# A filter contraction by channel quads, with selection matmuls in place of small relayout DMAs

## The chip, the cores and the metric

The kernel runs on one core of a Trainium2 chip. The metric is device time in microseconds (us); every time below is a median of three to seven runs. A profile gives the span of one run, which is about 1.8 us shorter than that run's time.

The runs fell on several chips, of two kinds. The kernel before took 367.5 to 368.0 us on two of them and 372.6 to 373.1 us on the others. So times of different sets are compared through the kernel before of the same set. A ratio is the mean time of one kernel's fast runs over that of the other's of the same rounds, so it is not quite the ratio of the medians that are quoted.

## The reference

Two branches share the input `u` (2048 x 640) and are mixed by a gate. Branch A builds a filter K for each of 640 channels from 128 complex modes and convolves it with `u` by way of spectra; branch B is a gated MLP.

```python
P = jnp.exp(logdA[:, :, None] * l[None, None, :])
K = jnp.einsum("dn,dnl,dn->dl", Cc, P, dB).real      # 640 channels x 2048
Kf = rfft(pad(K)); Uf = rfft(pad(u^T))               # cut: written with rfft2
y = irfft(Uf * Kf)[..., :L]^T + u * Dskip
b = (gelu(x @ w_gate) * (x @ w_up)) @ w_down
return g * y + (1 - g) * b
```

The kernel factors a position as l = X1 + X2, with 32 values of X1 and 21 of X2 (denser near the start, so K is computed at 672 points rather than at each of the 2048 positions), so that K of one channel is a 32 x 21 matrix, the product of a 128 x 32 and a 128 x 21 matrix over the 128 modes. There is a cosine and a sine part: two accumulating matmuls for each channel.

## The kernel before

All work is declared with a guessed duration and a lane (`pe` TensorE, `ac` ScalarE, `ve` VectorE, `dma` the Sync queue, `pool` GpSimd's). A planner then fixes the order on every engine from a `script` (the order of ScalarE's table functions) and a `prio` table (a priority for each lane). The order was found by search for this one kernel. Each engine and each DMA queue works strictly in its order.

The contraction, in chunks of 160 channels, four chunks, which run in two stretches of two:

```python
def contract(ch):
    c0 = CH * (ch % 2)
    for hb in range(2):
        def go(hb=hb):
            for g in range(GH):                       # 20
                for q in range(2):                    # cosine, sine
                    for j in range(4):                # one channel in each quarter of the columns
                        d = c0 + G4 * j + GH * hb + g
                        nc.tensor.matmul(ps[32 * j:32 * j + 32, 6 + hb, NX2 * g:NX2 * g + NX2],
                                         lhsT=cs1[ch % 2][:, q, :, d - c0],
                                         rhs=cs2[ch % 2][:, q, :, d - c0], start=(q == 0), stop=(q == 1))
        pe(160 * 20, go, ...)
    kst = at(O_KST + 1696 * (ch % 2), [128, NX2, G4], BF16, "kst")
    for hb in range(2):
        ac(actns(NX2 * GH), lambda hb=hb: nc.scalar.copy(...))          # PSUM to kst, 420 elements
    for j in range(4):
        for q in range(4):                                              # 16 small DMAs per chunk
            na = 6 if q == 0 else 5
            f = dma if j < 2 or ch < NCH - 1 else pool
            e = nc.sync if j < 2 or ch < NCH - 1 else nc.gpsimd
            f(410, lambda j=j, q=q, na=na, e=e: e.dma_start(
                out=Kt[32 * q:32 * q + 32, 0:na, CH * ch + G4 * j:CH * ch + G4 * j + G4],
                in_=kst[32 * j:32 * j + 32, q:NX2:4, :]), ..., lane="kt", prio=1)
```

`Kt` is the layout in which the spectrum matmuls read K. The Sync queue carries those DMAs (planned at 410 ns each), and also the MLP's weights, and the tables FK of K's spectrum:

```python
Wg = [at(O_W + 1280 * k, ...) for k in range(2)]
Wu = [at(O_W + 2560 + 1280 * k, ...) for k in range(2)]
... dma(430, go, w=[k], lane="w", x=KB160)                      # weights of MLP tile f
... dma(430, lambda i0=i0, n=n: nc.sync.dma_start(out=FK[:, i0:i0 + n]..., in_=dFK[...]), lane="fkl")
```

## Time and profile before

The kernel before takes 372.5 us (371.55 to 372.64). Its recorded profile has a span of 364.8 us, so its run took about 366.6 us. Where stages are compared in numbers, I therefore use two later runs on one and the same chip, called before_again (span 367.2) and after_again (span 349.4).

| kernel before, profile of span 364.8 us | |
|---|---|
| first contraction stretch | 106.3 to 123.4 us |
| second contraction stretch | 191.6 to 210.7 us |
| first K-spectrum matmul | 219.8 us |
| from there to the end (VectorE's spectrum products bind) | 145.0 us |

The page's costliest groups: busy us and the mean ns of one; then the idle time of the engine just before them and what ended it. The contraction's line has 1280 matmuls, with 15.2 us of idle time that no visible wait explains ("issue").

```profile
PE 304.6 (84%) x3014; PEld 180.6 (50%) x3014; DVE 297.8 (82%) x526; ACT 217.1 (60%) x333; POOL 21.2 (6%) x39
...
L514 PE MATMUL ps<-arena 128*32 128x21 bf16 x1280 | 21.0, 214 | 15.2 <-issue 15.2
```

TensorE's timeline in the first stretch (start, duration, then the idle time before in brackets) shows the shape of that idle time: after a first group of 240 pairs, 128 pairs of weight load and matmul, 256 instructions, take 2.1 us, and then nothing runs for 1.3 to 2.2 us.

```profile
106.28 3.71 PE L514 MATMUL ps<-arena 128*32 128x21 bf16 x240
111.28 2.14 PE L514 MATMUL ps<-arena 128*32 128x21 bf16 x128 [1.29 <-issue]
115.01 2.07 PE L514 MATMUL ps<-arena 128*32 128x21 bf16 x128 [1.59 <-issue]
118.74 2.09 PE L514 MATMUL ps<-arena 128*32 128x21 bf16 x128 [1.66 <-issue]
123.01 0.42 PE L514 MATMUL ps<-arena 128*32 128x21 bf16 x16 [2.19 <-issue]
```

The Trainium skill, "Advanced Engine Details and Errata", ISA Cache, gives an instruction cache line as 16 KB, 256 instructions. The trace agrees: the stops come every 256 instructions, and the instruction queue's transfers are 16 KB each (23 of them in this run).

The Sync queue's own timeline (L527 is the relayout DMA, L321 a weight load, L793 an FK load):

```profile
113.28 22.86 SPq L527 DMA_DIRECT2D arena<-arena  x32
136.24 0.54 SPq L321 DMA_DIRECT2D arena<-in_B_w_up_dram  x1
136.83 1.09 SPq L321 DMA_DIRECT2D arena<-in_B_w_gate_dram  x2
...
198.26 0.80 SPq L793 DMA_DIRECT2D arena<-dFK  x2
199.15 19.03 SPq L527 DMA_DIRECT2D arena<-arena  x24
218.22 1.06 SPq L793 DMA_DIRECT2D arena<-dFK  x2
```

The 32 relayout DMAs hold the queue for 22.86 us, 0.71 us each on average, not the planned 0.41. The waits between 124 and 182 us (engine, line, what it waited for: us in total, times, longest):

```profile
DVE arena L590 <- PE ps L586: 12.8, 10, 4.7
ACT arena L572 <- PE ps L568: 10.0, 10, 2.6
...
PE ps L568 <- DMA arena<-in_B_w_gate_dram: 2.8, 1, 2.8
```

### The profile page before, as it was taken

What the parts mean: (1) busy time and instruction counts of PE and PEld (TensorE: products, weight loads), DVE (VectorE), ACT (ScalarE), POOL (GpSimd) and SP (SyncE); (2) the same over time, 40 slices, a digit from 0 to 9 for tenths busy, and PEclk for the clock granted to TensorE, in tenths of its full rate; (3) what the DMA queues carried; (4) which work ended last, traced back from release to release, by engine and by line L of the source; (5) the groups of instructions that cost most, each with busy time, mean ns of one, the idle gap of its engine ahead of it and who ended that gap; (6) DMA issues with size and microseconds to landing.
All of it is one profiled execution on the core that took longest, in us unless ns stands there. A gap on an engine that the chain in (4) does not pass through costs nothing.

```text
span 364.8 us, 7365 instructions
## 1 busy us (share of the span) xinstructions
PE 304.6 (84%) x3014; PEld 180.6 (50%) x3014; DVE 297.8 (82%) x526; ACT 217.1 (60%) x333; POOL 21.2 (6%) x39
## 2 busy tenths in 40 slices
PE   0056669999995796999997397999999999999985
PEld 0012123444564442444446354667677777777654
DVE  8599599968893395898698613999999999998962
ACT  5899599999999567459991046999421011100000
POOL 6000000000000000000046050000000000000000
PEclk9999899999997598999997589999999999999999
DMA  7754523020200113020745524014520003001311
GB/s 151 191 102 102 133 115 106 18 55 20 56 20 13 21 21 73 2 55 18 217 151 142 162 32 161 2 39 136 101 44 2 18 20 90 20 18 46 102 65 62
DMA packets 63585, 26.42 MB, mean 72 GB/s; under 512 B 56832, under 2 KB 60864, under 8 KB 63168
## 3 DMA queue, kind: packets, MB, share of 16 engines
q1 hardware_dynamic: 62912, 24.54, 26.5%
q0 software_dynamic: 640, 1.42, 1.5%
q8 instruction: 23, 0.38, 0.4%
q14 instruction: 10, 0.08, 0.1%
HBM read 12.83 MB, written 6.03 MB: 52 GB/s over the span
## 4 chain that ended last, share of the span: by engine, by line
DVE 36%; PE 27%; ACT 18%; issue 8%; SPq 7%; DMA 3%; POOL 0%; DVEq 0%; ACTq 0%; POOLq 0%
DVE arena L881 28%; PE ps L586 9%; PE ps L568 7%; SPq L298 6%; PE ps L514 6%; ACT arena L461 4%; ACT arena L426 3%; ACT arena L572 3%; DVE arena L860 2%; PE ps L992 2%; DVE arena L1001 2%; ACT arena L361 2%; ACT arena L637 2%; PE ps L823 2%; ACT L572 1%
## 5 line engine op out<-in xcount | busy, mean ns | idle before, releaser
L881 DVE TENSOR_TENSOR arena<-arena 128x640 bf16<-128x640 bf16 (+5 forms) x112 | 106.6, 1006 | 2.3 <-ACT arena L975 0.9
L568 PE MATMUL ps<-arena 128*128 128x512 bf16 x280 | 70.7, 400 | 31.2 <-DMA arena<-in_A_u_dram 28.0
L586 PE MATMUL ps<-arena 128*128 128x512 bf16 x260 | 62.0, 389 | 0.5 <-DVE arena L590 0.4
L971 PE MATMUL ps<-arena 128*128 128x320 bf16 x448 | 62.0, 299 | 0.4 <-ACT arena L849 0.4
L568 PEld LDWEIGHTS <-arena 128*128 128x128 bf16 x280 | 28.2, 101 | 68.3 <-issue 32.4
L590 DVE TENSOR_TENSOR arena<-ps,arena 128x512 bf16<-128x512 f32 x52 | 35.0, 686 | 27.4 <-PE ps L586 26.4
L975 ACT ACTIVATE arena<-ps,omg 128x640 bf16<-128x640 f32 x16 | 12.7, 794 | 67.9 <-PE ps L971 61.0
L971 PEld LDWEIGHTS <-arena 128*128 128x128 bf16 x448 | 43.6, 98 | 17.2 <-issue 0.6
L461 ACT ACTIVATE arena<-arena 128x2240 bf16<-128x2240 int16 (+1 forms) x20 | 43.1, 2175 | 4.8 <-DVE arena L454 4.7
L586 PEld LDWEIGHTS <-arena 128*128 128x128 bf16 x260 | 25.9, 100 | 33.4 <-issue 5.3
L992 PE MATMUL ps<-arena 128*128 128x320 bf16 x256 | 37.7, 299 | 2.3 <-DVE arena L1001 1.2
L572 ACT ACTIVATE arena<-ps 128x512 bf16<-128x512 f32 (+1 forms) x56 | 29.2, 614 | 10.1 <-PE ps L568 10.0
L514 PE MATMUL ps<-arena 128*32 128x21 bf16 x1280 | 21.0, 214 | 15.2 <-issue 15.2
L992 PEld LDWEIGHTS <-arena 128*128 128x128 bf16 x256 | 24.7, 98 | 12.3 <-issue 3.3
L514 PEld LDWEIGHTS <-arena 128*32 128x32 bf16 x1280 | 20.0, 153 | 16.9 <-issue 16.9
L849 ACT CAST arena<-ps 128x640 bf16<-128x640 f32 (+1 forms) x40 | 21.2, 616 | 3.3 <-DVE arena L881 1.6
L452 DVE SCALAR_TENSOR_TENSOR arena<-arena 128x160 int32<-128x160 f32 x84 | 20.7, 316 | 2.0 <-ACT arena L461 2.0
L827 ACT ACTIVATE arena<-ps 128x640 bf16<-128x640 f32 x32 | 20.0, 805 | 3.8 <-PE ps L823 3.8
L843 PE MATMUL ps<-arena 128*128 128x320 bf16 x144 | 21.1, 299 | 1.2 <-ACT arena L849 0.5
L823 PE MATMUL ps<-arena 128*128 128x320 bf16 x128 | 20.4, 309 | 1.3 <-ACT arena L849 1.3
L785 POOL DMA_INDIRECT arena<-in_A_u_dram,i_u x8 | 9.5, 1190 | 181.9 <-ACT arena L461 179.8
L1001 DVE SCALAR_TENSOR_TENSOR arena<-ps,g_f,arena 128x640 bf16<-128x640 f32 x16 | 14.0, 876 | 6.5 <-PE ps L996 6.5
(87 smaller groups left out, 304.0 us busy)
## 6 DMA issues: line engine op xcount, KB each, us to landing
out_dram<-arena SPq DMA_DIRECT2D x16, 160.0 KB, 1.8
dFK<-arena SPq DMA_DIRECT2D x9, 256.0 KB, 2.0
arena<-in_B_w_gate_dram SPq DMA_DIRECT2D x13, 160.0 KB, 2.9
arena<-in_B_w_up_dram SPq DMA_DIRECT2D x13, 160.0 KB, 2.8
arena<-in_B_w_down_dram SPq DMA_DIRECT2D x13, 160.0 KB, 3.8
arena<-in_A_u_dram SPq DMA_DIRECT2D x4, 320.0 KB, 4.3
dTAB<-arena SPq DMA_DIRECT2D x1, 1024.0 KB, 4.3
arena<-dTAB SPq DMA_DIRECT2D x1, 1024.0 KB, 4.8
```

Source lines behind the costliest of these rows:

```text
L298: dma(1050, lambda: nc.sync.dma_start_transpose(out=xT[tq][:, kt, :], in_=u2[S * tq:S * tq + S, kt * 128:kt * 128 + 128]), w=[("xT", tq, k ...
L461: ac(actns(2 * n * w), lambda: nc.scalar.activation(out=dst, in_=ph.bitcast(I16)[:, :, :, 0:2 * w:2], func=ACT.Sin, scale=SIN_SCALE), r=[( ...
L514: nc.tensor.matmul(ps[32 * j:32 * j + 32, 6 + hb, NX2 * g:NX2 * g + NX2], lhsT=cs1[ch % 2][:, q, :, d - c0], rhs=cs2[ch % 2][:, q, :, d - ...
L568: nc.tensor.matmul(ps[:, k, :], lhsT=Wg[f % 2][:, kt, :], rhs=xT[tq][:, kt, :], start=(kt == 0), stop=(kt == NKT - 1))
L572: ac(actns(512), lambda: nc.scalar.activation(out=HT[f][0:p, tq, :], in_=ps[0:p, k, :], func=ACT.Gelu_apprx_tanh), r=[("bank", k)], w=[("H ...
L586: nc.tensor.matmul(ps[:, 4 + k, :], lhsT=Wu[f % 2][:, kt, :], rhs=xT[tq][:, kt, :], start=(kt == 0), stop=(kt == NKT - 1))
L590: ve(tt(512, 1) + 60, lambda: nc.vector.tensor_tensor(out=HT[f][:, tq, :], in0=ps[:, 4 + k, :], in1=HT[f][:, tq, :], op=ALU.mult), r=[("ba ...
L823: nc.tensor.matmul(ps[:, k + h, 0:DH], lhsT=tab[:, j, q, fsl(ft)], rhs=src[:, j, h * DH:(h + 1) * DH], start=(j == 0), stop=(j == 1))
L881: nc.vector.tensor_tensor(out=out, in0=a, in1=b, op=op)
L971: nc.tensor.matmul(ps[:, k + h, 0:DH], lhsT=HT[f][:, c, 128 * j:128 * j + 128], rhs=Wd[f][:, h * DH:(h + 1) * DH], start=(f == 0), stop=(f ...
L992: nc.tensor.matmul(ps[:, k + h, 0:DH], lhsT=tab[:, ft, q, 128 * j:128 * j + 128], rhs=U[ft][:, q, c, h * DH:(h + 1) * DH], start=(ft == 0 ...
L1001: ve(stt(640) + 50, lambda: nc.vector.scalar_tensor_tensor(out=osb[o].rearrange("p (h d) -> p h d", h=2), in0=ps[:, k:k + 2, 0:DH], scalar ...
```

## The change

The intent: channels k = 4g..4g+3 become one matmul pair, with all four channels' 32 columns as 128 columns of weights and all four channels' 21 columns as 84 moving columns. Of the 4 x 4 blocks of the result only the diagonal ones are wanted. There are 320 pairs in place of 1280. Each accumulator of five quads is copied to a staging tile, and 16 matmuls with 0/1 selection matrices (a "relay") pick the diagonal blocks and put them in `Kt`'s layout, from where two copies write `Kt`. No DMA is left in this path. All exponent, phase and sine tiles change to a quad-major layout for it, and the order (`script` and `prio`) was searched anew.

```diff
+    sj = cp.tile([128, 4, 32], BF16, name="sj")           # 0/1 selection
...
-    cs1 = [at(O_CS1 + 20480 * c, [128, 2, 32, CH], BF16, f"cs1{c}") for c in range(2)]
-    cs2 = [at(O_CS2 + 13440 * c, [128, 2, NX2, CH], BF16, f"cs2{c}") for c in range(2)]
+    cs1 = [at(O_CS1 + 20480 * c, [128, 2, NQD, 128], BF16, f"cs1{c}") for c in range(2)]
+    cs2 = [at(O_CS2 + 13440 * c, [128, 2, NQD, 4 * NX2], BF16, f"cs2{c}") for c in range(2)]
... (exponentials, phases, sines and products write and read the new layout: cut)
-            (the contraction, two copies and 16 DMAs per chunk, shown above)
+    kst = at(O_KST, [128, 4 * NX2, NQD // 2], BF16, "kst")
+        for h in range(2):
+            for s in range(4):
+                def go(k=k, k0=k0):
+                    for g in range(5):
+                        for q in range(2):
+                            nc.tensor.matmul(ps[:, k, 84 * g:84 * g + 84], lhsT=cs1[c][:, q, k0 + g, :],
+                                             rhs=cs2[c][:, q, k0 + g, :], start=(q == 0), stop=(q == 1))
+                pe(10 * 38, go, ...)
+                ac(actns(420), lambda k=k, s=s: nc.scalar.copy(
+                    out=kst[:, :, 5 * s:5 * s + 5], in_=ps[:, k, 0:420].rearrange("p (g e) -> p e g", e=84)), ...)
+            def relay(k=k):
+                for q in range(4):
+                    na = 6 if q == 0 else 5
+                    for j in range(4):
+                        o = ps[32 * q:32 * q + 32, k, 0:480].rearrange("p (a j g) -> p a j g", a=6, j=4)[:, 0:na, j, :]
+                        nc.tensor.matmul(o, lhsT=sj[:, j, :], rhs=kst[:, 4 * q + j:4 * NX2:16, :], start=True, stop=True)
+            def back(k=k, ds=ds):
+                for p, a0, a1 in ((128, 0, 5), (32, 5, 6)):
+                    nc.scalar.copy(out=Kt[0:p, a0:a1, ds]..., in_=ps[0:p, k, 80 * a0:80 * a1]...)
...
-    script = [("trig", 8), ("exp", 6), ("sqrt", 1), ...]
-    prio = {("ACT", "copy"): 2, ..., ("PE", "gate"): 7, ("PE", "k"): 3, ("SP", "w"): 8, ...}
+    script = [("exp", 1), ("trig", 9), ("exp", 5), ("sqrt", 1), ...]
+    prio = {("ACT", "copy"): 1, ..., ("PE", "gate"): 0, ("PE", "k"): 4, ("SP", "w"): 3, ...}
```

## The prediction

> **What bounds the kernel now.** The chain of waits, in order of time, shows: 44 to 88 us mostly ScalarE table functions and copies; 88 to 158 us nearly all TensorE (gate, up, K contraction); 159 to 186 us ScalarE again (sine, gelu, exp, table loads); 191.6 to 220 us the second K contraction and its hand-over. From 226 us VectorE's spectrum products bind; the change leaves that tail alone.
>
> The 1280 contraction matmuls (weights 128x32, 21 columns) occupy TensorE from 106.3 to 123.4 us and from 191.6 to 210.7 us (timeline), 36 us, although they run at 16 ns each: 128 take 2.07 us and are followed by 1.3 to 4.1 us of "issue" (groups by line: 15.2 us in all). I read these gaps as instruction supply, 256 instructions per stop. The second contraction is followed by small relayout DMAs, which hold the Sync queue for 19.0 us (199.2 to 218.2) and push the FK table's loads behind them. First K-spectrum matmul: 219.8 us.
>
> **Removed.** 1280 pairs become 320, with full 128-column weights and 84 columns. The Trainium skill, "TensorE: Matmul & The Clock Gate", Back-to-back issue gap, gives N/2.4 + 2.5 ns; the trace agrees for 320 columns (16 matmuls in 2.17 us, 136 ns). Estimate: 37.5 ns each, 12 us in all, too slow a rate for instruction supply to bind. The 64 DMAs go.
>
> **Added.** 128 selection matmuls, about 1 us per relay of 16 (estimate from about 105 columns), 8 us. ScalarE: 24 more PSUM copies of 420 elements at 506 ns (12.1 us) and 8 writes back, about 0.7 us each (5.7 us, estimated from the copies). TensorE loses about 16 us, ScalarE gains 18 us. Element counts stay; I expect VectorE and ScalarE means unchanged within 5% (inner runs of four keep 8 bytes together).
>
> **How much is critical.** TensorE was nearly saturated from 42 to 191.6 us; there about 5 us are saved (17.2 to 12), but ScalarE, 97% busy from 80 to 120 us, takes 9 us of new work; it has slack only from 120 to 160 us (63% busy). So the second contraction should start 3 us earlier, at about 188 us. It becomes a serial loop between TensorE and ScalarE: four copies, relay, write back, with one staging tile and two PSUM banks, about 4.6 us per half chunk, 18 us for four, 23 us where the clock falls to half: hardly shorter than 19.0 us. The gain comes after it: about 5.5 us to the first K-spectrum matmul in place of 9.1. Sum: 3 + (19.0 - 20) + 3.6 + 1 for FK, so 6 to 7 us.
>
> **Predicted:** 366 us, 8 in 10 within 358.5 to 372.5. Faster by over 2%: 0.43; within 2%: 0.52; slower by over 2%: 0.05.
>
> **What would show it.** Contraction pairs at 37 to 45 ns without 1.3 us issue gaps; ScalarE busy up by 17 to 19 us; first K-spectrum matmul at 210 to 216 us; the tail after it within 2 us of 145 us; in the last contraction ScalarE waiting 1.2 to 2 us for each relay. Exponential (454 ns), sine (2065, 2339 ns) and product (1314, 1486 ns) means unchanged.
>
> **What would make it wrong.** Runs of four slowing ScalarE or VectorE (106 exponentials: 20% would be 10 us of ScalarE); half clock through the whole last contraction; TensorE queued behind a 2 us sine for a bank; or a re-tuned order that hides the copies completely (10 to 14 us faster).

## The result, and the profile after

The kernel after takes 357.86 us (357.65 to 358.82), the kernel before 372.57 us in the same rounds: ratio 0.9619, 95% interval 0.9591 to 0.9648. The result is correct. That is 14.7 us of gain, where 6.5 was predicted.

| us from the span's start | before_again | after_again | difference | predicted |
|---|---|---|---|---|
| second contraction starts | 192.4 | 182.0 | -10.4 | -3 |
| its length, to the last matmul (before) or write back to Kt (after) | 19.9 | 17.6 | -2.3 | +1 |
| from there to the first K-spectrum matmul | 9.9 | 6.1 | -3.8 | -3.6 |
| from there to the end | 145.0 | 143.7 | -1.3 | -1 (FK) |
| span | 367.2 | 349.4 | -17.8 | -6.5 |

Both traces are of one chip; the medians there are 367.61 and 351.18 us, and the run of before that was traced was a slower one of its set. The second contraction's start on TensorE's timeline, before_again and then after_again:

```profile
192.40 3.45 PE L514 MATMUL ps<-arena 128*32 128x21 bf16 x216
```

```profile
182.03 0.92 PE L524 MATMUL ps<-arena 128*128 128x84 bf16 x20
```

The answering lines of the page after, first of its costliest groups. L529 is the staging copy; its mean was to be 506 ns.

```profile
PE 299.7 (84%) x2182; PEld 175.8 (49%) x2182; DVE 297.8 (84%) x528; ACT 237.2 (67%) x374; POOL 15.7 (4%) x32
...
L529 ACT CAST arena<-ps 128x420 bf16<-128x420 f32 x32 | 20.3, 674 | 10.9 <-PE ps L524 6.9
```

TensorE's timeline in the first stretch: pieces of the contraction (L524) and relays (L540) alternate with the MLP's matmuls (L606), and no idle time is listed.

```profile
111.25 0.92 PE L524 MATMUL ps<-arena 128*128 128x84 bf16 x20
112.00 2.45 PE L606 MATMUL ps<-arena 128*128 128x512 bf16 x10
114.59 0.40 PE L540 MATMUL ps<-arena,sj 128*32 128x120 bf16 x16
114.92 0.55 PE L524 MATMUL ps<-arena 128*128 128x84 bf16 x10
```

Twenty contraction matmuls take 0.92 us and ten 0.54 to 0.55, so one more takes (0.92 - 0.55) / 10 = 37 ns. The Trainium skill, "TensorE: Matmul & The Clock Gate", Back-to-back issue gap, gives N/2.4 + 2.5 ns for the gap of an isolated matmul, 37.5 ns for 84 columns, and warns that it counts too little for pairs with weight loads (81 ns at 128 columns). These are such pairs, and the trace keeps to the formula without that addition.

The Sync queue: weights (L325) go out when their buffers are free, and the FK loads (L816) are not behind anything.

```profile
113.27 6.96 SPq L325 DMA_DIRECT2D arena<-in_B_w_up_dram  x2
120.28 1.35 SPq L325 DMA_DIRECT2D arena<-in_B_w_gate_dram  x2
127.32 11.69 SPq L325 DMA_DIRECT2D arena<-in_B_w_up_dram  x2
...
194.35 2.60 SPq L816 DMA_DIRECT2D arena<-dFK  x4
```

The waits between 124 and 182 us: the wait for gate weights is down to 0.4 us (on the weight-load side; it was 3.8 there before), and the gelu's wait for TensorE, 10.0 us before, is no longer listed.

```profile
ACT arena L529 <- PE ps L524: 1.2, 3, 0.6
...
PEld L588 <- DMA arena<-in_B_w_gate_dram: 0.4, 1, 0.4
```

The same stretches in windows, first before_again, then after_again (window, its length, then busy us of TensorE, its weight loads, VectorE, ScalarE, GpSimd; the granted clock; DMA share; GB/s). From 137 to 182 us ScalarE was busy 33.54 of 45 us before, and 44.81 after: the new order fills it.

```profile
109.00:137.00 28.00, 20.94 (x524) 13.02 (x520) 16.41 (x38) 20.43 (x27) 0.00 (x0) 0.76 0.14 17
137.00:182.00 45.00, 41.17 (x181) 17.96 (x182) 35.06 (x75) 33.54 (x46) 0.00 (x0) 0.96 0.29 74
```

```profile
109.00:137.00 28.00, 27.44 (x311) 15.46 (x315) 25.74 (x62) 24.70 (x35) 0.00 (x0) 1.00 0.14 31
137.00:182.00 45.00, 41.85 (x186) 18.44 (x189) 41.74 (x82) 44.81 (x61) 4.01 (x4) 1.00 0.33 90
```

Summed from 60 us to the start of the second contraction, ScalarE's idle time falls from 20.0 us (of 132.4) to 3.9 us (of 122.0), although it does 5.7 us more work there.

The serial loop of the second contraction is as it was foreseen, in after_again: copy, matmuls, relay, write back (L547), at full clock.

```profile
188.57 0.54 PE L524 MATMUL ps<-arena 128*128 128x84 bf16 x10 [0.47 <-ACT arena L529]
189.20 0.71 ACT L529 CAST arena<-ps 128x420 bf16<-128x420 f32 x1 [0.17 <-PE ps L524]
189.96 0.40 PE L540 MATMUL ps<-arena,sj 128*32 128x120 bf16 x16 [0.85 <-ACT arena L529]
190.29 0.55 PE L524 MATMUL ps<-arena 128*128 128x84 bf16 x10
190.47 0.60 ACT L547 CAST arena<-ps 128x400 bf16<-128x400 f32 x2 [0.56 <-PE ps L540]
```

### The profile page after: what moved, and what is told of

It is laid out like the page before. It is cut to its first block, busy times and chain, and to the rows that moved or that the text cites. A ratio compares the mean times of both kernels' runs of the same rounds, so it can differ in the third digit from the quotient of the medians.

```text
span 355.9 us, 5682 instructions
## 1 busy us (share of the span) xinstructions
PE 299.7 (84%) x2182; PEld 175.8 (49%) x2182; DVE 297.8 (84%) x528; ACT 237.2 (67%) x374; POOL 15.7 (4%) x32
## 4 chain that ended last, share of the span: by engine, by line
DVE 38%; PE 27%; ACT 19%; SPq 10%; issue 4%; DMA 1%; another core or an unknown queue 0%; DVEq 0%; ACTq 0%
DVE arena L904 28%; PE ps L588 10%; PE ps L606 8%; SPq L302 7%; ACT arena L466 5%; ACT arena L529 3%; PE ps L524 3%; DVE arena L883 3%; ACT arena L592 3%; PE ps L1015 2%; ACT arena L430 2%; SPq L307 2%; DVE arena L1024 2%; PE ps L846 2%; ACT arena L660 2%
## 5 line engine op out<-in xcount | busy, mean ns | idle before, releaser
L588 PE MATMUL ps<-arena 128*128 128x512 bf16 x280 | 68.5, 396 | 25.9 <-DMA arena<-in_B_w_gate_dram 21.8
L606 PE MATMUL ps<-arena 128*128 128x512 bf16 x260 | 62.3, 382 | 3.2 <-DVE arena L610 3.0
L588 PEld LDWEIGHTS <-arena 128*128 128x128 bf16 x280 | 27.9, 101 | 61.7 <-DMA arena<-in_B_w_gate_dram 22.2
L994 PEld LDWEIGHTS <-arena 128*128 128x128 bf16 x448 | 43.6, 98 | 17.2 <-issue 0.6
L606 PEld LDWEIGHTS <-arena 128*128 128x128 bf16 x260 | 24.8, 99 | 33.4 <-issue 7.2
L1015 PEld LDWEIGHTS <-arena 128*128 128x128 bf16 x256 | 24.7, 98 | 12.7 <-issue 3.7
L529 ACT CAST arena<-ps 128x420 bf16<-128x420 f32 x32 | 20.3, 674 | 10.9 <-PE ps L524 6.9
L420 ACT ACTIVATE arena<-arena 128x320 bf16<-128x320 f32 x64 | 23.3, 465 | 0.0
L883 DVE TENSOR_TENSOR arena<-arena 128x640 bf16<-128x640 bf16 (+1 forms) x30 | 11.1, 419 | 12.9 <-ACT arena L872 12.9
L850 ACT ACTIVATE arena<-ps 128x640 bf16<-128x640 f32 x32 | 20.1, 813 | 1.6 <-PE ps L846 1.6
L655 PE MATMUL ps<-arena 128*128 128x512 bf16 x42 | 13.6, 450 | 8.6 <-ACT arena L660 8.1
```

Source lines behind the costliest of these rows:

```text
L420: nc.scalar.activation(out=e1[:, :, 4 * r:4 * r + 4], in_=quads(aT[:, ds]), func=ACT.Exp, scale=float(sg * (4 + 8 * i)))
L529: ac(actns(420), lambda k=k, s=s: nc.scalar.copy(out=kst[:, :, 5 * s:5 * s + 5], in_=ps[:, k, 0:420].rearrange("p (g e) -> p e g", e=84)), ...
L588: nc.tensor.matmul(ps[:, k, :], lhsT=Wg[f % 2][:, kt, :], rhs=xT[tq][:, kt, :], start=(kt == 0), stop=(kt == NKT - 1))
L606: nc.tensor.matmul(ps[:, 4 + k, :], lhsT=Wu[f % 2][:, kt, :], rhs=xT[tq][:, kt, :], start=(kt == 0), stop=(kt == NKT - 1))
L994: nc.tensor.matmul(ps[:, k + h, 0:DH], lhsT=HT[f][:, c, 128 * j:128 * j + 128], rhs=Wd[f][:, h * DH:(h + 1) * DH], start=(f == 0), stop=(f ...
L1015: nc.tensor.matmul(ps[:, k + h, 0:DH], lhsT=tab[:, ft, q, 128 * j:128 * j + 128], rhs=U[ft][:, q, c, h * DH:(h + 1) * DH], start=(ft == 0 ...
```

## The experiments

The first question was where the surplus of 8 us came from. Two theories: the new contraction alone made the gain (A), or the new order alone did (C).

### Same chip: both kernels, and each half of the change alone

before_again and after_again are the two kernels, unchanged, to have both traces from one chip.

> The kernel before, unchanged, to get a second trace. Its timed runs give 372.5 us, but its first trace has a span of 364.8 us, while the changed kernel's time is only 1.8 us over its span. So the first trace should not show an ordinary run. Theory A (instruction supply): time 372, span 370 to 371, and the 6 us more than in the first trace lie in the two stretches of contraction matmuls, which together take 41 to 43 us in place of 36. Theory B (another place: start, clock or the tail): the two stretches take 35 to 37 us and the 6 us are found before 106 us or after the first K-spectrum matmul.

Measured: 367.85 us, ratio 0.9998 (0.9934 to 1.0061). Neither theory's time came: this chip was faster, and the two stretches take 17.2 + 19.9 = 37.1 us.

> The changed kernel, unchanged, on the same chip: 357.5 to 359 us, span 1.8 us less, first K-spectrum matmul at 212 to 214 us. Both theories expect this; a second trace shows how far its stages move from run to run.

Measured: 351.18 us, ratio 0.9555 (0.9494 to 0.9616): 6 us below what was expected, and the first K-spectrum matmul comes at 205.7 us, not at 212 to 214.

new_k_old_order has the new contraction with the old script and priorities; old_k_new_order is the reverse:

```diff
# new_k_old_order, against after
-    script = [("exp", 1), ("trig", 9), ...];  prio = {...}      # new
+    script = [("trig", 8), ("exp", 6), ...];  prio = {...}      # old
# old_k_new_order, against before
-    script, prio: old
+    script, prio: new, and ("POOL", "kt"): 6, ("SP", "kt"): 5 for the relayout DMAs
```

> The new contraction and relay with the old ScalarE script and the old lane priorities. Theory A (the contraction itself made the gain): 358 to 363 us. Theory C (the re-tuned order made most of it): 367 to 373 us, since ScalarE's 18 us of new copies then stand in an order made without them.

Measured: 372.52 us, ratio 1.0128 (1.0051 to 1.0205). The second contraction starts at 203.4 us, 11.0 later than before; ScalarE's idle time ahead of it stays at 19.8 us (20.0 before) while its work grows by 11.2 us.

> The old contraction and its DMAs with the new script and priorities. Theory A: 370 to 376 us, no better than before. Theory C: 360 to 366 us.

Measured: 378.02 us, ratio 1.0259 (1.0184 to 1.0335). The second contraction starts at 200.2 us. ScalarE's idle time ahead of it is 29.4 us.

So each half alone loses 5 and 10 us, and both together win 16. Neither theory holds by itself. One rival was not tested: each order was searched for its own kernel, and no run shows what a further search with the old contraction would win.

### One part of the order alone

```diff
# new_k_old_script_new_prio, against after          # new_k_new_script_old_prio, against after
-    script = [new]                                 -    prio = {new}
+    script = [old]                                 +    prio = {old}
```

> The new contraction, the old ScalarE script, the new lane priorities. The whole order was worth 21 us on the new contraction (372.5 against 351.2 us). Theory: the script is what fills ScalarE, so this stays near the old order, 365 to 373 us, ratio 0.99 to 1.015. Rival: the priorities did it, 351 to 358 us, ratio below 0.975.

Measured: 383.17 us, ratio 1.027 (1.0242 to 1.0298); second contraction from 214.2 us. That is slower than either expectation.

> The new contraction, the new script, the old priorities. Theory (script): within 6 us of the changed kernel, ratio 0.955 to 0.975. Rival (priorities): 365 us or more, ratio over 0.99. If both mixed kernels are slow, script and priorities only work together.

Measured: 373.86 us, ratio 1.0047 (0.9996 to 1.0097); second contraction from 200.1 us. With both mixed kernels slow, script and priorities also win only together.

### Which engine is full after the change

copies_twice makes every staging copy twice, matmuls_twice every contraction matmul.

```diff
# copies_twice
-                ac(actns(420), lambda k=k, s=s: nc.scalar.copy(...), ...)
+                def stage(k=k, s=s):
+                    for _ in range(2):
+                        nc.scalar.copy(...)
+                ac(actns(420), stage, ...)
# matmuls_twice
-                    for g in range(5):
+                    for g in [x for y in range(5) for x in (y, y)]:
```

> The changed kernel with each of its 32 staging copies made twice (same values, same order, planned as before). It adds 32 times about 0.5 us = 16 us to ScalarE alone, half of it before the second contraction. Theory S (ScalarE has no slack left from 60 us to the K spectrum): 14 to 18 us over the changed kernel, a ratio to before of 0.995 to 1.01, and the second contraction starts 7 to 9 us later than 182 us. Theory T (TensorE bounds the middle and ScalarE still has slack there): 8 to 10 us, ratio 0.978 to 0.988, and the second contraction starts within 3 us of 182 us.

Measured: 375.07 us, ratio 1.0067 (1.0046 to 1.0088), so 17 us over after (357.86 on the same kind of chip) for 20.4 us more ScalarE work (busy 257.6 in place of 237.2). The second contraction starts 9 us later.

> The changed kernel with each of its 320 contraction matmuls made twice (same result, same order). It adds 12 us to TensorE alone, 6 us before the second contraction. Theory S: 1 to 5 us over the changed kernel, ratio to before 0.96 to 0.972. Theory T: 8 to 12 us, ratio 0.978 to 0.99.

Measured: 367.38 us, ratio 0.9866 (0.9836 to 0.9895), 9.5 us over after for about 12 us more TensorE work (an estimate: 320 times the 37 ns read above). The second contraction starts 6 us later.

Both hold: neither engine has much room for more work. That doubling a cost hurts does not show that halving it helps, as the next runs proved.

### Shorter staging copies

The staging copy takes 674 ns and not the 506 ns of the copy before. It writes runs of five elements, the old one runs of 20. plain_staging lets it write one contiguous run; the relay's matmuls then read with a stride.

```diff
-    kst = at(O_KST, [128, 4 * NX2, NQD // 2], BF16, "kst")
+    kst = at(O_KST, [128, NQD // 2, 4 * NX2], BF16, "kst")
-                    out=kst[:, :, 5 * s:5 * s + 5], in_=ps[:, k, 0:420].rearrange("p (g e) -> p e g", e=84)),
+                    out=kst[:, 5 * s:5 * s + 5, :], in_=ps[:, k, 0:420].rearrange("p (g e) -> p g e", e=84)),
-   rhs=kst[:, 4 * q + j:4 * NX2:16, :]
+   rhs=kst[:, :, 4 * q + j:4 * NX2:16].rearrange("p g a -> p a g")
```

> The kernel after, with the staging tile laid out quad-major, so that each of the 32 staging copies writes one contiguous run of 420 elements (it reads the accumulators in their order) and the relay's matmuls read the tile with a stride. Theory: the copy's extra length (674 ns measured against 506 ns of the copy it replaced) comes from its strided access; the mean falls to 480-560 ns, ScalarE loses some 4 to 6 us of work, and as ScalarE has no slack before the second contraction the time falls by 3 to 5 us against the kernel after (ratio to before 0.948 to 0.956 where after gives 0.962; 0.943 to 0.949 on a chip where after gives 0.9555). Rival: the relay's 16 matmuls, 0.40 us with contiguous columns, slow to over 1 us with strided ones and sit in the serial loop, or the copy stays above 600 ns: no gain over 1 us.

Measured: 359.68 us, ratio 0.9661 (0.9595 to 0.9726): no gain. The copies took 508 ns, as the theory had it, but the rival is right: a relay takes 1.06 us in place of 0.40. staging_by_fives keeps both short, with one block of the staging tile for each copy, contiguous, in which the relay finds its runs of five:

```diff
-    kst = at(O_KST, [128, 4 * NX2, NQD // 2], BF16, "kst")
+    kst = at(O_KST, [128, 4, 4 * NX2, 5], BF16, "kst")
-                    out=kst[:, :, 5 * s:5 * s + 5], ...
+                    out=kst[:, s, :, :], ...
-   rhs=kst[:, 4 * q + j:4 * NX2:16, :]
+   rhs=kst[:, :, 4 * q + j:4 * NX2:16, :].rearrange("p s a g -> p a s g")
```

It ran with the kernel after beside it on one chip (after_third), which is the base of that set.

> The kernel after, unchanged, on the chip of the runs beside it, as their base: ratio to before 0.955 to 0.963.

Measured: 351.38 us (350.67 to 353.29), ratio 0.9558 (0.9483 to 0.9633).

> The kernel after, with the staging tile in four blocks, one for each staging copy: each copy writes one contiguous run of 420 elements (508 ns in plain_staging), and the relay's matmuls still read runs of five neighbouring elements, as they do after. Theory that the copy's short runs cost 0.17 us each and that ScalarE has no slack: copies at 500-520 ns, a set of 16 relay matmuls stays at 0.40-0.45 us, and the time falls by 3 to 5 us against the kernel after on this chip (two copies a half lie on the serial path of the last contraction, 16 before it are in the full stretch). Rival that TensorE's order alone sets the second contraction's start: 0 to 1.5 us. Third outcome, relay matmuls slow again because their runs are now split in four: over 0.8 us a set and no gain.

Measured: 349.85 us (348.74 to 351.46), ratio 0.9498 (0.942 to 0.9576): 1.5 us faster than after_third by the medians, and the ranges overlap. The groups show the copy of plain_staging and of staging_by_fives, in this order:

```profile
L529 ACT CAST arena<-ps 128x420 bf16<-128x420 f32 x32 | 15.4, 508 | 14.0 <-PE ps L524 9.7 <-issue 2.5 <-remote 1.7
```

```profile
L529 ACT CAST arena<-ps 128x420 bf16<-128x420 f32 x32 | 15.2, 507 | 7.6 <-PE ps L524 7.3
```

and TensorE's timeline one relay of each, again in this order:

```profile
205.73 1.06 PE L540 MATMUL ps<-arena,sj 128*32 128x120 bf16 x16 [0.65 <-ACT arena L529]
```

```profile
197.72 0.47 PE L540 MATMUL ps<-arena,sj 128*32 128x120 bf16 x16 [0.65 <-ACT arena L529]
```

The copy of staging_by_fives still reads its accumulator with a stride, so it is the short written runs that cost, not the reading. But the expectation of 3 to 5 us for 5 us less ScalarE work was too high. The windows suggest why. In the first contraction's stretch (109 to 137 us) TensorE is the full engine (27.44 of 28 us, ScalarE 24.70); ScalarE is full only after it (44.81 of 45 us), where no staging copy lies. The copies' saved time in the first stretch becomes idle time (ScalarE 23.07 us busy in staging_by_fives) and the second contraction starts only 0.6 us earlier. Adding 10.8 us of copies there overflows the 3.3 us of room; taking 2.7 us away wins nothing. In the second contraction the write back ends 1.3 us earlier (198.9 us; 200.2 in after_third), but the first K-spectrum matmul only 0.1 us: between them, TensorE's spectrum matmuls of `u` take turns with ScalarE's copies of them.

### Accumulator banks and VectorE's help after the second contraction

four_banks lets the first spectrum stages rotate through four pairs of accumulator banks where they had two. helps_banks2 does this and moves some of their copies to VectorE, which is idle there.

```diff
# both
-                k = two(4 if ft else 2)
+                k = two(4 if ft or b else 2)
-                k = two(4 if ft or 1 in hs else 2)
+                k = two(4)
# helps_banks2 also
+                if ft == 0 and q == 1:
+                    ve(tt(640, 1) + 60, lambda ...: nc.vector.tensor_scalar(out=dst, in0=src2, scalar1=1.0 / S, ...), lane="kcp", ...)
+                on_v = ft == 0 and hs == [0] and q == 1           # and the K-spectrum's copies likewise
```

> The kernel after, with a few accumulator copies of the first spectrum stages moved from ScalarE to VectorE where that is idle before its first product (about 12.8 us), and four accumulator pairs in rotation instead of two there. Theory that ScalarE and TensorE together are the limit before the second contraction, without slack: ScalarE work of about 5 us goes away, TensorE waits less for banks; the time falls by 2 to 4 us against the kernel after. Rival: the same order of heads is bound by something else (VectorE's products), no gain: within 1 us of after.

Measured: 353.78 us, ratio 0.9486 (0.9425 to 0.9548), against 0.9619 (357.86 us) for after on the same kind of chip: 4 us faster by the medians, 5 by the ratios. That is a little more than expected, and in another place: the second contraction starts no earlier (184.1 us; 182.6 after). The time is won behind it: from its start to the first K-spectrum matmul 26.1 us (29.6 after), and 142.3 us from there to the end (143.8 after).

> The kernel after, with four accumulator pairs in rotation instead of two for two of the spectrum stages, nothing moved to VectorE. If the banks alone made the gain of helps_banks2 (about 4 to 5 us against after): 3 to 5 us faster than after. If VectorE's share of the copies made it: within 1 us of after.

Measured: 349.25 us, ratio 0.9483 (0.9412 to 0.9555), 2.1 us under after_third: between the two expectations. The banks alone give about half; that VectorE's copies give the rest is inferred across two kinds of chip, and no run moves the copies alone.

### What the old contraction cost in the old order

before_half_contraction leaves out half of the contraction's matmuls. It gives a wrong filter.

```diff
-                    for q in range(2):
+                    for q in range(1):
-                                             ..., start=(q == 0), stop=(q == 1))
+                                             ..., start=True, stop=True)
```

> The kernel before with half of the contraction matmuls of each channel left out (wrong result on purpose), order and all else unchanged. If the contraction's own time is paced by the number of its instructions, its two stretches fall from 17 and 19 us to about 8.5 and 10 us, the idle time that the contraction's line shows with no named wait falls from 15-16 us to 7-8 us, and as the stretches' instructions are shared with the heads' work only part is on the chain. Theory that the old contraction held up the whole TensorE order: the time falls by 14 to 18 us (ratio 0.953 to 0.962). Rival, that only the last stretch is on the chain: by 9 to 11 us (ratio 0.970 to 0.976).

Measured: 367.66 us, ratio 0.9858 (0.9786 to 0.993), 5.4 us: both expectations were too high. The first stretch fell from 17.2 to 8.7 us and the second from 19.9 to 12.2. The first has the expected size, but 3.8 us of it is now a wait for ScalarE's copy. The idle time without a named wait fell over both only from 16.1 to 13.5 us (7 to 8 expected): on this slower kind of chip the second stretch is cut into bursts of some five matmuls. It starts only 2.2 us earlier, and although the first K-spectrum matmul comes 11.9 us earlier (210.3 us), most of that is lost again at once. Lines of the chain of waits (start, duration, what) show it: relayout DMAs (SPq L527), one after another, stand before the FK load (L793), and TensorE's next K-spectrum matmuls wait for that table.

```profile
212.43 0.36 SPq L527
...
216.72 0.60 SPq L527
217.36 0.59 SPq L793
218.00 4.05 DMA arena<-dFK
```

TensorE's wait for FK there is 8.8 us (on the weight-load side 9.7, against 0.5 in before_again). (This kernel's outputs still passed the comparison with the reference, so that comparison says little about the filter.)

### The relayout DMAs as the cost

before_one_dma issues one DMA per chunk in place of 16, moving about the same bytes to wrong places (relative error 0.05).

```diff
+                def one(j=j, q=q):
+                    if j == q == 0:
+                        nc.sync.dma_start(out=Kt[:, 0:5, CH * ch:CH * ch + CH], in_=<800 elements of kst>)
-                f(410, lambda ...: e.dma_start(...), ...)
+                f(410, one, ...)
```

> The kernel before with one relayout DMA per chunk in place of 16 (wrong result on purpose; the bytes moved are about the same, the issues are 4 and not 64). Theory: the issue of 16 DMAs by one engine after the last chunk is most of the 9 us from the contraction's end to the first K-spectrum matmul; it falls to 5 to 7 us and the time by 2 to 4 us (ratio 0.989 to 0.995). Rival: the latency of one DMA is the term, and the issues overlap it: 0 to 1 us.

Measured: 366.59 us, ratio 0.985 (0.9782 to 0.9918): 6.5 us by the medians, more than either expected, and in another place. The hand-over after the second contraction did not shorten (10.2 us; 9.9 before). The second contraction starts at 185.2 us in place of 192.4, because the weight loads which stood behind 32 DMAs until 137.3 us in before_again go out from 127.0 us. Most of these 7.2 us are not kept: the second contraction takes 24.0 us (19.9 in before_again), and the first K-spectrum matmul comes only 2.8 us earlier. This run is of the slower kind of chip, of which there is no trace of the kernel before, so the stages compare only roughly. And the amount of DMAs changed too. before_gpsimd_relayout separates the two: all 64 DMAs stay, on another queue, and the result is right. The order on TensorE, VectorE and ScalarE is unchanged.

```diff
-                e = nc.sync if j < 2 or ch < NCH - 1 else nc.gpsimd
+                e = nc.gpsimd
```

> The kernel before, all 64 relayout DMAs issued from GpSimd's queue and none from Sync's; the order of every compute engine is the same as before, the result is right. Theory that the DMAs cost time by holding the Sync queue, with the weight loads behind them: the weight loads that were issued at 137.3 us come 10 to 20 us earlier, TensorE's wait for gate weights there (3.6 us) goes, the second contraction starts at 184 to 188 us, and the time falls by 3 to 6 us (ratio 0.984 to 0.992; the last chunk's 16 DMAs on one queue may give 2 us back at the hand-over). Rival that the DMAs' traffic of small packets, or their number, is the cost: no earlier start, ratio 0.996 or more.

Measured: 362.03 us (361.29 to 363.02) against 367.49, ratio 0.9832 (0.9771 to 0.9892). The theory holds, though the weight loads come 8.2 us earlier (129.1 for 137.3) and not 10 to 20. The timelines of the Sync and the GpSimd queue, then TensorE's wait for gate weights from 124 to 182 us, in before_again and in this run:

```profile
105.63 23.84 SPq L321 DMA_DIRECT2D arena<-in_B_w_up_dram  x2
129.51 6.45 SPq L321 DMA_DIRECT2D arena<-in_B_w_gate_dram  x2
```

```profile
113.97 9.53 POOL L527 DMA_DIRECT2D arena<-arena  x16 [107.17 <-ACT arena L519]
123.94 9.60 POOL L527 DMA_DIRECT2D arena<-arena  x16 [0.43 <-ACT arena L519]
```

```profile
PEld L568 <- DMA arena<-in_B_w_gate_dram: 4.6, 2, 4.1
```

```profile
PEld L568 <- DMA arena<-in_B_w_gate_dram: 0.6, 1, 0.6
```

TensorE's weight loads waited 4.6 us for gate weights in before_again and wait 0.6 us here; the second contraction starts at 187.2 us, 5.2 earlier. A change of one line in the kernel before wins 5.5 us. The Trainium skill, "Perfetto Trace Analysis", DMA Optimizations, advises spreading DMAs over the engines that can issue them when issuing is the limit; this run agrees.

old_k_new_order_one_dma asks whether the same DMAs are why the old contraction did badly in the new order: old_k_new_order with the edit of before_one_dma.

> The old contraction in the new order (1.026 of before), with one relayout DMA per chunk in place of 16 (wrong result on purpose). Theory that the Sync queue is also what made the new order worse with the old contraction: the second contraction starts over 8 us earlier than 200.2 us and the ratio falls to 0.99 to 1.00. Rival that the stops of the contraction on TensorE do it: starts within 4 us of 200.2, ratio above 1.015.

Measured: 372.82 us, ratio 1.0122 (1.0052 to 1.0191); the second contraction starts at 194.0 us, 6.2 earlier. This lies between the two expectations: the DMAs are a good part of it, not the whole. (This edit removes DMAs, so it does not separate the queue from their number.)

### A version that beats both

fives_helps joins staging_by_fives and helps_banks2.

> helps_banks2 with the staging tile in four blocks. If both gains add: 3 to 5 us under helps_banks2's distance to after, so 6 to 9 us faster than after on this chip (ratio to before 0.936 to 0.945). If both take the same slack away: 4 to 5 us faster than after, as helps_banks2 alone.

Measured: 345.72 us (345.48 to 346.41), ratio 0.9391 (0.9321 to 0.946), correct: 22 us faster than before and 5.7 us faster than after_third on the same chip. This lies between the two expectations by the medians, and within what was expected if the gains add by the ratio. The first K-spectrum matmul comes at 201.7 us (205.5 in after_third).

## Why the prediction was wrong, point by point

- **The failed step** is "So the second contraction should start 3 us earlier, at about 188 us." It started 10.4 us earlier on one chip (192.4 to 182.0), and at 182.6 in the run with the recorded times. This one term makes up 7.4 of the missing 11.3 us in the traced pair.
- **First cause: a cost that was not counted.** The prediction saw the relayout DMAs hold the Sync queue after the second contraction (199.2 to 218.2 us). The same timeline has 32 of them from 113.3 to 136.1 us, with the MLP's weights behind. "The 64 DMAs go" was worth nothing in its sum at that place. before_gpsimd_relayout shows 5.2 us of earlier start and 5.5 us of time for the queue alone, with contraction and the order of TensorE, VectorE and ScalarE untouched.
- **Second cause: an idle time taken as given.** "It has slack only from 120 to 160 us" was true of the old order. The prediction kept that order's idle time and listed "a re-tuned order that hides the copies completely (10 to 14 us faster)" as what would make it wrong. ScalarE's idle time ahead of the second contraction went from 20.0 to 3.9 us. On the new contraction, the order moved the second contraction's start from 203.4 to 182.0 us. The order alone does not do it: with the old contraction ScalarE's idle time was 29.4 us. That it needs the short pieces of the new contraction is likely, but no run tests them alone. How the 10.4 us divide between the two causes is not settled, as they do not add: the new contraction in the old order lost its DMAs too and started later.
- **A third share was not tested: the clock.** TensorE was granted half clock (0.50 and 0.51) in before_again from 113.8 to 127.5 and from 141.1 to 144.6 us, and full clock in after_again from 60 to 182 us. Two groups of MLP matmuls that lie partly in those stretches took 7.17 us (24 matmuls) and 5.10 us (15), where 20 took 4.48 us between the stretches: about 3.5 us of TensorE time (an estimate from these). No run holds the clock fixed.
- **The loop** was mis-sized: 20 us predicted, 17.6 measured in after_again. Its upper half, a falling clock, did not come (1.00 in that loop), and a relay takes 0.40 us at full clock, where 1 us was estimated. That is at most 25 ns for each of the 16 matmuls, less than the 46 ns that the formula above would give for 105 columns (an estimate); no run asks why. In the run with the recorded times the loop took 23.4 us, with half clock from 190.0 to 193.4 us and the stop told below. The hand-over (-3.8 against -3.6) and the tail were right.
- **The mechanism of the contraction was right**: 37 ns per pair, no stops every 256 instructions, ScalarE's work up by 20.1 us (17 to 19 predicted; the copies' 674 ns instead of 506 is 32 x 0.168 = 5.4 us of it, with the relays' write backs at 0.70 us as estimated). The means of exponential (453 to 465 ns), sine (2077 and 2343) and product (1316 and 1484) did not move by more than 3%.
- **One hit is luck.** The first K-spectrum matmul came at 212.1 us in the run with the recorded times (210 to 216 predicted). But the prediction started from a trace that is presumably of the faster kind of chip, and there it came at 205.7 us: too early a start and a slower chip cancelled.
- **The size of the copy** looked like a costly miss and was not: made short again it won 1.5 us at best.

One thing stays open. On the slower kind of chip the second contraction lasts longer (182.6 to 204.1 us after, against 182.0 to 197.6 for its matmuls in after_again). In that stretch ScalarE, VectorE and TensorE each stop for some 2.9 to 3.5 us between 185 and 191 us while GpSimd issues indirect loads. The profile names "remote" or "issue" as releasers, and a like stop is in plain_staging and helps_banks2. In before_one_dma, on the same kind of chip, the old contraction comes there in bursts of about five matmuls with "issue" between them, which before_again does not show. Most of the 6.7 us between the two kinds of chip lies between the second contraction's start and the first K-spectrum matmul (29.6 against 23.7 us), and no run tells its cause.

## What to carry to other kernels

When small DMAs are replaced, look at every place where they hold a queue and at what stands behind them, not only at the place where their data are awaited; moving them to an idle queue is a one-line test, and here was worth a third of the gain. When a change comes with a new order, idle time of the old order is not a constant: add up the work of each engine up to the next join and ask which engine would be full in which stretch. And a cost that hurts when it is doubled may still be worth nothing when it is taken away.

## What the Trainium skill lacked or had wrong

- "DMA: Bandwidth & Descriptors", Where the ~2 µs actually goes, gives about 50 ns for the sequencer's dispatch of a DMA (in a table for the GpSimd path), and Issuing engines are not separate DMA queues says that spreading DMAs over engines saves only the time it takes to initiate them, "usually small relative to the DMA itself". Here one relayout DMA held its queue for 0.58 us on GpSimd and 0.60 us on Sync (medians), a third of its 1.9 to 2.0 us from issue to landing, and putting them on GpSimd's queue saved 5.5 us of 367.5.
- The same page, SWDGE vs HWDGE vs iDMA, calls the hardware path (Sync) faster to set up than the software path (GpSimd). The issue of these DMAs does not show it: 576 ns on GpSimd in before_gpsimd_relayout against 602 ns on Sync in before_again (medians).
- "SBUF — State Buffer", Door 1: The DMA port swizzle, says that accesses which cross to a new 16-byte line pay a penalty, with no size. Measured: a ScalarE copy of 420 bf16 elements took 674 ns with written runs of five elements (10 bytes) and 507 to 508 ns when it wrote contiguously; 16 matmuls whose moving elements lie 168 bytes apart took 1.06 us, with runs of five 0.47, with runs of twenty 0.40.
- No page has the stop of three engines, 2.9 to 3.5 us each, that some runs on the slower kind of chip show and no run of the kernel after on the faster kind (second contraction 21.5 against 15.6 us for the same matmuls).
